# Which queue issues the first loads: both first x tiles and a quarter of Wq from ScalarE, and eight V stores moved behind Wo's loads

## The chip, the cores and the metric

The kernel runs on one core of a Trainium2 chip. The core has TensorE (PE, matrix products), VectorE (DVE), ScalarE (ACT), GpSimd (POOL) and SyncE (SP). SyncE, ScalarE and GpSimd can issue DMAs; each has a queue of its own, and the 16 DMA engines of the core serve all of them. The metric is the device time of one execution in microseconds (us), lower is better. Unless another unit is given, numbers in the text are microseconds, and points in time are counted from the start of the profiled span.

## The reference

A segment-recurrent attention block, then a gated block with spatial mixing, on one sequence of S = 2048 rows, width 512, 32 heads of 128, 64 segments of 32 rows, and 8 memory rows that each segment hands to the next:

```python
x = layernorm(A_x)
mem = mem0
for s in range(64):
    h = concat([mem, x[:, 32*s:32*s+32]])          # 40 rows
    q, k, v = h @ Wq, h @ Wk, h @ Wv               # 32 heads of 128
    p = softmax(where(mask, q @ k.T * 128**-0.5, -1e9))
    o = sum over heads of (p @ v) @ Wo
    mem = o[:, :8]
    outs.append(o[:, 8:])
h = A_x + concat(outs)
z = gelu(layernorm(h) @ w_in)
g = w_sp @ layernorm(z[:, 896:]) + b_sp
out = h + (z[:, :896] * g) @ w_out
```

## The kernel before

The program is recorded operation by operation by a small emitter. It keeps one list for each engine, in the order in which the calls are made, and works out from tokens (names of buffers that an operation reads or writes) which semaphore each one waits for. So the order of the calls is the order on each engine, and a DMA stands in the queue of the engine whose list it was added to (`sp(...)` for SyncE, `em.add("act", ..., dma=True)` for ScalarE, `"pool"` for GpSimd). These parts are enough to follow what is said below:

- **First loads** (lines 300 to 323). `load_xe(ck, j)` (L300) loads an "x end" tile of 128 x 512 in bf16: the last 8 rows of each of the 16 segments of chunk `ck`. `load_x(rb, j)` (L292) loads a block of 128 rows of x. `load_w(mi, hq, queues)` (L310) loads quarter `hq` (8 heads, 1 MB) of Wq, Wk or Wv (`mi` 0, 1, 2); with two queues named it is cut into two halves of 512 columns, each a DMA of its own with a token of its own, so that readers of the first four heads wait for the first half alone. A row of a half is 1 KB for each of 4 x 128 descriptors, a row of a whole quarter 2 KB. L315 loads ScalarE's table for exp and ln.
- **The start of the work** (lines 797 to 848). 34 small matmuls warm TensorE up (`warm`, L794). The two x tiles get their layernorm: statistics of both on VectorE (L363, L364), then the scale (L373). The first is transposed on TensorE (L383) and copied to `hTe` by ScalarE (L407). Then come 16 groups of `start_x` (L445): `start_x(ck, i)` gives q of the segment ends of chunk `ck` for heads 4i to 4i + 3 (i below 8; from 8 on it gives k). The order is `start_x(0, 0)`, the transposes of the second tile, then `start_x(0, 1)`, `start_x(1, 0)`, `start_x(0, 2)`, `start_x(1, 1)` and so on. `start_x(0, 0)` and `start_x(1, 0)` read the first half of Wq's first quarter, `start_x(0, 1)` and `start_x(1, 1)` the second half, each further pair of i one more quarter. PSUM results go alternately through ScalarE (L461) and VectorE (L463).
- **The batched V groups** (L472). Eight groups `start_v(n)` give v of the segment ends of chunk 0. `vx_evac` (L476 to L490) copies a group to `part[n]` (L484 on ScalarE for odd n, L486 on VectorE for even n) and stores it to DRAM (`vext_d`) in two pieces: the first 16 of its 128 rows, which segments 0 and 1 need, from ScalarE's or GpSimd's queue, and the other 112 rows from SyncE's queue. The `part` buffers are written again by `part_evac` (L684) from segment 0 on, and that has to wait for the stores.
- **Wo's loads** (L852): four DMAs of 1 MB on SyncE's queue, with no wait of their own. They are read by L672 from the end of segment 0 on.
- **The segments** (from L940): 64 rounds. `load_vx(s)` (L497) fetches the stored V rows of one segment, for segments 0 and 1 from GpSimd's queue; for the others SyncE does it, two segments ahead, and waits for all 16 store pieces. The rows are used in L645.

After the segments come the second block's products (L1163 spatial mixing, L1258 output).

Of the kernel before, what the change touches and what calls it, by code (L numbers as in the profile page):

```python
# [169 lines left out]
def fast_path(nc, st, keep, A_x, A_mem0, A_Wq, A_Wk, A_Wv, A_Wo, A_seg_len, B_w_in, B_w_sp, B_b_sp, B_w_out, out):  # L170
# [25 lines left out]
    em = Emitter(n_dma_sems=40)  # L196
# [71 lines left out]
    def PB(b):  # L268
        return ("ps", b)

    def sp(fn, **k):
        return em.add("sp", fn, dma=True, **k)
# [4 lines left out]
    def act(fn, **k):  # L277
        return em.add("act", fn, **k)

    def dve(fn, **k):  # L280
        return em.add("dve", fn, **k)
# [8 lines left out]
    def load_x(rb, j):  # L290
        t, tok = xbuf(j)
        sp(lambda e: e.dma_start(t, xr[:, rb, :]), writes=tok)  # L292


    def xbuf(j):
        return (xn[:, j, :], [("xn", j)]) if j < 2 else (part[:, j, :], [("part", j, 0), ("part", j, 1)])

    def load_xe(ck, j, queue="sp"):
        t, tok = xbuf(j)
        em.add(queue, lambda e: e.dma_start(t, xe[CK * ck:CK * ck + CK, XM:SEG, :]), dma=True, writes=tok)  # L300

    def load_w(mi, hq, queues=("sp",)):
        parts = len(queues)
        wd, ws = ((A_Wq, w_q), (A_Wk, w_k), (A_Wv, w_v))[mi]
        wr = wd.rearrange("(dc p) h e -> p dc (h e)", p=128)
        n = 8 * DH // parts
        for k in range(parts):
            c0, c1 = hq * 8 * DH + k * n, hq * 8 * DH + (k + 1) * n
            tok = ("W", mi, hq) if k == parts - 1 else ("W", mi, hq, k)
            em.add(queues[k], lambda e, c0=c0, c1=c1: e.dma_start(ws[:, :, c0:c1], wr[:, :, c0:c1]), dma=True, writes=[tok])  # L310
            em.mark_const(tok)

    load_xe(0, 0)
    load_xe(1, 1, "act")
    act(lambda e: e.preload_act_table_set("natural_log_exp_and_others"))  # L315
    load_w(0, 0, ("sp", "sp"))
    load_w(0, 1, ("act",))
    load_w(0, 2)
    load_w(0, 3, ("act",))
    load_x(0, 4)  # L320
    load_x(1, 5)
    load_xe(2, 6)
# [153 lines left out]
    def vx_evac(ck, n, bank, eng="act", queue="sp"):  # L476
        if ck == 0:
            t, tok = part[:, n, :], [("part", n, 0), ("part", n, 1)]
        else:
            j = vcnt[0] % 2  # L480
            vcnt[0] += 1
            t, tok = Vs[:, j, :], [("Vs", j)]
        if eng == "act":
            act(lambda e: e.activation(out=t, in_=ps[:, bank, :], func=ACT.Copy, scale=VSC), reads=[PB(bank)], writes=tok)  # L484
        else:
            dve(lambda e: e.tensor_scalar(out=t, in0=ps[:, bank, :], scalar1=VSC, scalar2=None, op0=ALU.mult), reads=[PB(bank)], writes=tok)  # L486
        for k, (i0, i1) in enumerate(((0, 2), (2, CK)) if ck == 0 else ((0, CK),)):
            r = slice(8 * i0, 8 * i1)
            dst = vext_d[ck, n, r, :, :].rearrange("p r e -> p (r e)")
            em.add("sp" if k else queue, lambda e, r=r, dst=dst: e.dma_start(dst, t[r, :]), dma=True, reads=tok, writes=[("vext", ck, n, k)])  # L490

    vcnt = [0]
    NVL = 2

    def load_vx(s, queue="sp"):
# [278 lines left out]
    def zp_evac(rb, hf, bank, eng):  # L774
        j = zpc[0] % 2
        zpc[0] += 1
        t = Vs[:, j, 0:HF]
        if eng == "act":
            act(lambda e: e.activation(out=t, in_=ps[:, bank, 0:HF], func=ACT.Copy), reads=[PB(bank)], writes=[("Vs", j)])
        else:  # L780
            dve(lambda e: e.tensor_copy(out=t, in_=ps[:, bank, 0:HF]), reads=[PB(bank)], writes=[("Vs", j)])
        sp(lambda e: e.dma_start(zp_d[rb, :, hf * HF:(hf + 1) * HF], t), reads=[("Vs", j)], writes=[("zpd", rb, hf)])
# [39 lines left out]
    def start_v(n, ck=0):  # L822
        start_group(vx_mm, vx_evac, ck, n)
# [27 lines left out]
    for hq in range(4):  # L851
        sp(lambda e, hq=hq: e.dma_start(w_o[:, 8 * hq:8 * hq + 8, :], wor[:, 8 * hq:8 * hq + 8, :]), writes=[("Wo", hq)])  # L852
        em.mark_const(("Wo", hq))

    class Gap:
        def __init__(self):
# [22 lines left out]
    def vx_group(ck, n):  # L879
        gx.append([lambda dc=dc: vx_mm(ck, n, XB, dc) for dc in range(DC)] + [lambda: vx_evac(ck, n, XB, "dve")])  # L880

    def vx_atoms(ck, n):
        mms = [lambda ck=ck, n=n, dc=dc: vx_mm(ck, n, VXB, dc) for dc in range(DC)]
        gv.add(VXB, mms, lambda eng: vx_evac(ck, n, VXB, eng))
# [55 lines left out]
    for s in range(NSEG):  # L940
# [89 lines left out]
        if s == 3 * CK + 1:  # L1030
            for r, hf in zgap:
                gv.add(VXB, [lambda r=r, hf=hf, dc=dc: zp_mm(r, hf, VXB, (dc,)) for dc in range(DC)],
                       lambda eng, r=r, hf=hf: zp_evac(r, hf, VXB, eng))
# [142 lines left out]
    def zbank():  # L1176
        zcnt[0] += 1
        return 5 + zcnt[0] % 3
# [26 lines left out]
    for i, rb in enumerate(order):  # L1205
# [23 lines left out]
        if i in (3, 4):  # L1229
            r, j, bank = RB - 5 + i, i % 2, zbank()  # L1230
# [729 lines left out]
def build_kernel(nc, A_x, A_mem0, A_Wq, A_Wk, A_Wv, A_Wo, A_seg_len, B_x, B_w_in, B_w_sp, B_b_sp, B_w_out, out):  # L1960
    args = (A_x, A_mem0, A_Wq, A_Wk, A_Wv, A_Wo, A_seg_len, B_w_in, B_w_sp, B_b_sp, B_w_out, out)
    with contextlib.ExitStack() as keep:
        with contextlib.ExitStack() as st:
            em, sems, dsems, flag = fast_path(nc, st, keep, *args)
# [88 lines left out]
```

## Time and profile before

| | |
|---|---|
| device time, median of 3 runs (lowest to highest) | 863.92 us (863.6 to 864.41) |
| the profiled execution | 861.39 us |
| its span, first to last instruction | 859.8 us |
| mean granted TensorE clock | 0.995 |
| busy: PE, ACT, DVE, POOL | 98%, 57%, 53%, 19% of the span |
| DMA | 76.09 MB, mean 88 GB/s; 327 and 385 GB/s in the first two slices of 21.5 us |

How to read it: in the timeline a row has its start, its length (of several merged instructions from the first start to the last end), the engine, the line of the kernel, the operation, what it writes and reads, how many were merged, and in brackets the idle time of the engine before it with what ended that. "SPq" and "ACTq" are DMA issues on SyncE's and ScalarE's queue; the length is that of the issuing instruction, not of the transfer. Matmuls are pipelined, so a busy TensorE is not one at its peak. In the table of DMA queues a row has the queue, its packets, its MB and the time that its packets took as a share of 16 engines' time; q1 is SyncE's queue, q10 ScalarE's, q0 GpSimd's.

### The profile page before, as it was taken

What the parts mean: (1) busy time and instruction counts of PE and PEld (TensorE: products, weight loads), DVE (VectorE), ACT (ScalarE), POOL (GpSimd) and SP (SyncE); (2) the same over time, 40 slices, a digit from 0 to 9 for tenths busy, and PEclk for the clock granted to TensorE, in tenths of its full rate; (3) what the DMA queues carried; (4) which work ended last, traced back from release to release, by engine and by line L of the source; (5) the groups of instructions that cost most, each with busy time, mean ns of one, the idle gap of its engine ahead of it and who ended that gap; (6) DMA issues with size and microseconds to landing.
All of it is one profiled execution on the core that took longest, in us unless ns stands there. A gap on an engine that the chain in (4) does not pass through costs nothing.

```text
span 859.8 us, 48647 instructions
## 1 busy us (share of the span) xinstructions
PE 843.7 (98%) x22466; PEld 495.2 (58%) x22466; DVE 455.2 (53%) x1031; ACT 492.8 (57%) x1309; POOL 160.0 (19%) x409
## 2 busy tenths in 40 slices
PE   7999999999999999999999999999999999999997
PEld 7755665566565665656565556565665544444443
DVE  3545545555555555565556555555555466563443
ACT  2466676766776676667776667666666676300000
POOL 4212112111221111111211121112211123200000
PEclk8999999999999999999999999999999999999999
DMA  9972212131312230213112120433332289023001
GB/s 327 385 217 68 66 47 59 48 77 32 71 39 43 57 78 24 70 55 65 58 49 69 25 78 26 119 70 75 69 76 63 68 249 318 1 98 107 35 13 47
DMA packets 95730, 76.09 MB, mean 88 GB/s; under 512 B 46040, under 2 KB 81504, under 8 KB 95520
## 3 DMA queue, kind: packets, MB, share of 16 engines
q1 hardware_dynamic: 93632, 70.09, 28.6%
q8 instruction: 178, 2.92, 1.5%
q10 hardware_dynamic: 1616, 2.49, 0.8%
q0 software_dynamic: 272, 0.33, 0.1%
q14 instruction: 32, 0.26, 0.1%
HBM read 41.75 MB, written 20.91 MB: 73 GB/s over the span
## 4 chain that ended last, share of the span: by engine, by line
PE 95%; DMA 2%; SPq 1%; ACT 1%; DVE 1%; issue 0%; ACTq 0%; POOL 0%; DVEq 0%; POOLq 0%
PE f_ps L523 26%; PE f_ps L672 13%; PE f_ps L618 13%; PE f_ps L1163 11%; PE f_ps L422 4%; PE f_ps L472 4%; PE f_ps L717 3%; PE f_ps L1258 3%; PE f_ps L638 3%; PE f_ps L445 2%; PE f_ps L563 2%; PE f_ps L768 2%; PE f_ps L1156 2%; DMA f_arena<-in_A_Wq_dram 1%; PE f_ps L555 1%; PE f_ps L584 1%
## 5 line engine op out<-in xcount | busy, mean ns | idle before, releaser
L523 PE MATMUL f_ps<-f_arena,f_hT 128*32 128x512 bf16 (+1 forms) x5120 | 241.1, 337 | 0.2
L534 ACT ACTIVATE f_Tst<-f_ps 128x512 bf16<-128x512 f32 (+1 forms) x320 | 150.1, 510 | 46.8 <-PE f_ps L523 40.3
L523 PEld LDWEIGHTS f_ps<-f_arena,f_hT 128*32 128x32 bf16 x5120 | 119.8, 96 | 93.0 <-ACT f_hT L695 34.8
L618 PE MATMUL f_ps<-f_arena,f_hT 128*32 128x512 bf16 x2048 | 139.0, 379 | 0.0
L672 PE MATMUL f_ps<-f_arena,f_cT 128*32 128x256 bf16 x4096 | 128.3, 272 | 1.2 <-issue 1.0
L608 POOL TENSOR_TENSOR f_E_sb<-f_R_sb,f_E_sb 128x64 bf16<-128x64 f32 x128 | 52.7, 412 | 380.6 <-ACT f_R_sb L600 380.6
L542 DVE STREAM_TRANSPOSE f_QT<-f_Tst 128x256 uint32<-128x256 uint32 x128 | 57.0, 445 | 124.0 <-ACT f_Tst L534 124.0
L672 PEld LDWEIGHTS f_ps<-f_arena,f_cT 128*32 128x32 bf16 x4096 | 99.7, 96 | 23.8 <-ACT f_cT L658 20.5
L1163 PE MATMUL f_ps<-f_arena 128*128 128x512 bf16 x448 | 100.6, 379 | 0.6 <-DMA f_arena<-wT_d 0.6
L660 DVE TENSOR_SCALAR f_cT<-f_ps 128x320 bf16<-128x320 f32 x128 | 56.9, 486 | 46.3 <-PE f_ps L645 46.3
L1163 PEld LDWEIGHTS f_ps<-f_arena 128*128 128x128 bf16 x448 | 43.7, 98 | 53.1 <-DMA f_arena<-wT_d 0.7
L684 ACT ACTIVATE f_part<-f_ps 128x256 bf16<-128x256 f32 x128 | 49.2, 384 | 39.6 <-PE f_ps L672 37.3
L542 DVE STREAM_TRANSPOSE f_KT<-f_Tst 128x128 uint32<-128x128 uint32 (+1 forms) x192 | 65.8, 343 | 7.0 <-ACT f_Tst L534 2.9
L630 DVE TENSOR_SCALAR f_V_sb<-f_ps 128x512 bf16<-128x512 f32 x64 | 44.3, 692 | 47.1 <-PE f_ps L618 47.1
L658 ACT ACTIVATE f_cT<-f_ps 128x320 bf16<-128x320 f32 x128 | 49.0, 435 | 34.2 <-PE f_ps L645 34.2
L577 ACT ACTIVATE f_E_sb<-f_ps 128x224 bf16<-128x224 f32 x128 | 45.4, 354 | 35.0 <-PE f_ps L569 34.1
L604 DVE TENSOR_TENSOR f_E_sb<-f_R_sb,f_E_sb 128x160 bf16<-128x160 f32 x128 | 41.7, 325 | 18.5 <-ACT f_R_sb L600 18.5
L695 ACT ACTIVATE f_hT<-f_ps 128x16 bf16<-128x16 f32 x126 | 23.2, 184 | 45.0 <-PE f_ps L692 45.0
L618 PEld LDWEIGHTS f_ps<-f_arena,f_hT 128*32 128x32 bf16 x2048 | 40.0, 96 | 14.8 <-issue 0.3
L1169 DVE TENSOR_TENSOR f_arena<-f_ps,f_arena 128x512 f32<-128x512 f32 x28 | 19.3, 690 | 52.7 <-PE f_ps L1163 52.7
L600 ACT ACTIVATE f_R_sb<-f_R_sb 128x160 f32<-128x160 f32 x128 | 43.1, 337 | 4.5 <-ACT f_Vs L484 0.4
L422 PE MATMUL f_ps<-f_arena,f_hTe 128*32 128x512 bf16 x640 | 41.6, 379 | 0.0
(124 smaller groups left out, 1152.7 us busy)
## 6 DMA issues: line engine op xcount, KB each, us to landing
wT_d<-f_wst SPq DMA_DIRECT2D x32, 256.0 KB, 3.7
f_arena<-wT_d SPq DMA_DIRECT2D x32, 256.0 KB, 5.5
f_arena<-in_A_Wv_dram SPq DMA_DIRECT2D x4, 1024.0 KB, 11.8
f_arena<-in_A_Wk_dram SPq DMA_DIRECT2D x4, 1024.0 KB
f_arena<-in_A_Wo_dram SPq DMA_DIRECT2D x4, 1024.0 KB, 12.0
f_Vx<-vext_d SPq DMA_DIRECT2D x62, 64.0 KB
vext_d<-f_Vs SPq DMA_DIRECT2D x22, 128.0 KB, 2.0
zp_d<-f_Vs SPq DMA_DIRECT2D x20, 112.0 KB, 2.1
```

The costliest lines, as they stand in the source:

```text
L422: pe(lambda e, c=c, rhs=rhs: e.matmul(ps[32 * c:32 * c + 32, bank, :], lhsT=hTe[:, ck, dc, 32 * sg:32 * sg + 32], rhs=rhs, start=(dc == 0) ...
L523: pe(lambda e, dc=dc, c=c, rhs=rhs: e.matmul(ps[32 * c:32 * c + 32, bank, 0:32 * nh], lhsT=hT[:, sl, dc, :], rhs=rhs, start=(dc == 0), sto ...
L534: act(lambda e: e.activation(out=st_.rearrange("p (hp i r) -> p hp i r", i=32, r=2), in_=ps[:, bank, 0:64 * np_].rearrange("p (hp r i) -> ...
L542: dve(lambda e: e.transpose(out=dst, in_=src), reads=tok, writes=[(nm, b, k) for k in halves(b, p0, np_)])
L577: act(lambda e: e.activation(out=E_sb[:, b, :], in_=ps[:, bank, 0:224], func=ACT.Exp, scale=scale, bias=SHIFT), reads=[PB(bank)], writes=[ ...
L608: pool(lambda e: e.tensor_tensor(out=ev, in0=rv, in1=ev, op=ALU.mult), reads=[("R", b), ("Ex", b)], writes=[("Ex", b)])
L618: pe(lambda e, dc=dc, c=c, c0=c0: e.matmul(ps[32 * c:32 * c + 32, bank, 0:w], lhsT=hT[:, sl, dc, :], rhs=w_v[:, dc, c0:c0 + w], start=(dc ...
L658: act(lambda e: e.activation(out=dst, in_=src, func=ACT.Copy, scale=UNSC), reads=[PB(PVB[c])], writes=[("cT", c)])
L660: dve(lambda e: e.tensor_scalar(out=dst, in0=src, scalar1=UNSC, scalar2=None, op0=ALU.mult), reads=[PB(PVB[c])], writes=[("cT", c)])
L672: pe(lambda e, h=h, g=g, i=i, b=b, c=c: e.matmul(ps[32 * g:32 * g + 32, bank, 0:d1 - d0], lhsT=cTh[:, i, 8:40], rhs=w_o[:, h, d0:d1], star ...
L684: act(lambda e: e.activation(out=part[:, s % 8, d0:d1], in_=ps[:, bank, 0:d1 - d0], func=ACT.Copy), reads=[PB(bank)], writes=[("part", s % ...
L1163: pe(lambda e: e.matmul(ps[:, bank, 0:TB], lhsT=z2[:, sc, fb * 128:(fb + 1) * 128], rhs=wTb[tb % 2][:, :, sc, :], start=first, stop=last), ...
```

## The change

Two things are changed. The products, their order on TensorE, VectorE, ScalarE and GpSimd, and the bytes that are moved are the same.

First, the first loads. Before, SyncE's queue had x tile 0, the two halves of Wq's first quarter, and Wq's third quarter; ScalarE's queue had x tile 1, the table load, Wq's second and fourth quarter. Now ScalarE's queue has x tile 0, x tile 1, the two halves of Wq's first quarter, and then the table load; SyncE's queue starts with Wq's second, third and fourth quarter. What follows on SyncE's queue (three more x blocks, `mem0`, Wv, Wk) keeps its order.

Second, the 112-row stores of the V groups. They are put on a list (`vrest`) when the group is copied and are added to SyncE's queue behind Wo's four loads. The 16-row stores are where they were.

```diff
-    load_xe(0, 0)
+    load_xe(0, 0, "act")
     load_xe(1, 1, "act")
+    load_w(0, 0, ("act", "act"))
     act(lambda e: e.preload_act_table_set("natural_log_exp_and_others"))
-    load_w(0, 0, ("sp", "sp"))
-    load_w(0, 1, ("act",))
-    load_w(0, 2)
-    load_w(0, 3, ("act",))
+    for hq in range(1, 4):
+        load_w(0, hq)
     load_x(0, 4)
     load_x(1, 5)
     load_xe(2, 6)
...
-            em.add("sp" if k else queue, lambda e, r=r, dst=dst: e.dma_start(dst, t[r, :]), dma=True, reads=tok, writes=[("vext", ck, n, k)])
-
-    vcnt = [0]
+            if k:
+                vrest.append(lambda r=r, dst=dst: sp(lambda e: e.dma_start(dst, t[r, :]), reads=tok, writes=[("vext", ck, n, 1)]))
+            else:
+                em.add(queue, lambda e, r=r, dst=dst: e.dma_start(dst, t[r, :]), dma=True, reads=tok, writes=[("vext", ck, n, 0)])
+
+    vcnt, vrest = [0], []
...
     for hq in range(4):
         sp(lambda e, hq=hq: e.dma_start(w_o[:, 8 * hq:8 * hq + 8, :], wor[:, 8 * hq:8 * hq + 8, :]), writes=[("Wo", hq)])
         em.mark_const(("Wo", hq))
+    for f in vrest:
+        f()
```

## The prediction

> **What bounds the kernel now.** I read the page first, then the chain of waits, then the timeline of the start, the packets of each DMA queue in short windows, and the granted clock by window.
>
> ```profile
> span 859.8 us, 48647 instructions
> ...
> PE 95%; DMA 2%; SPq 1%; ACT 1%; DVE 1%; issue 0%; ACTq 0%; POOL 0%; DVEq 0%; POOLq 0%
> ```
>
> The chain that ended last runs on TensorE for 95% of the span; 2% of it are DMAs. The chain in order of time shows the long one:
>
> ```profile
> 1.56 9.46 DMA f_arena<-in_A_Wq_dram
> ...
> 28.79 7.02 PE f_ps L472 x128
> ```
>
> So the transfer on the path is the first half of Wq's first quarter (I call the halves Wq0a and Wq0b), on its way from 1.56 to 11.02. The change touches the start only, and what it does to the start is carried to the end: in that chain no other DMA stands between 11.02 and the V groups (L472). The timeline of the start:
>
> ```profile
> 0.81 0.69 SPq L300 DMA_DIRECT2D f_xn<-in_A_x_dram  x1
> 0.82 0.67 ACTq L300 DMA_DIRECT2D f_xn<-in_A_x_dram  x1
> 1.56 1.11 ACTq L310 DMA_DIRECT2D f_arena<-in_A_Wq_dram  x2
> 1.56 1.98 SPq L310 DMA_DIRECT2D f_arena<-in_A_Wq_dram  x3
> 4.00 0.69 DVE L363 BATCH_NORM_STATS2 f_st<-f_xn 128x6 f32<-128x512 bf16 x1 [4.00 <-DMA f_xn<-in_A_x_dram]
> 4.83 0.66 DVE L363 BATCH_NORM_STATS2 f_st<-f_xn 128x6 f32<-128x512 bf16 x1
> 6.82 0.60 ACT L407 ACTIVATE f_hTe<-f_ps 128x512 bf16<-128x512 bf16 x1 [4.02 <-PE f_ps L383]
> 11.15 1.87 PE L445 MATMUL f_ps<-f_hTe,f_arena 128*128 128x128 bf16 x16 [3.82 <-DMA f_arena<-in_A_Wq_dram]
> 13.24 13.80 PE L445 MATMUL f_ps<-f_hTe,f_arena 128*128 128x128 bf16 x224
> ```
>
> Two x tiles go to VectorE's statistics (both, before the first is applied), the first tile's transpose is ready at 6.82 + 0.60 = 7.42, and TensorE then waits 3.7 us for Wq0a. The first group (16 matmuls, heads 0 to 3) takes 1.87 us; after the second tile's transposes the second group starts at 13.24. That one reads heads 4 to 7, so it needs **Wq0b**, and from there 224 matmuls run without a hole. So 13.24 is the time to beat, and the transfer that decides it after the change is Wq0b, not Wq0a.
>
> **How the queues share.** Packets by queue (q10 is ScalarE's, q1 SyncE's), in the windows 2 to 3.5, 3.5 to 5, 7 to 10, 11 to 12 and 0 to 12 us, in this order:
>
> ```profile
> q10 hardware_dynamic: 154, 0.15, 54.6%
> q1 hardware_dynamic: 127, 0.12, 23.0%
> ...
> q10 hardware_dynamic: 238, 0.49, 90.1%
> q1 hardware_dynamic: 17, 0.01, 2.3%
> ...
> q10 hardware_dynamic: 371, 0.76, 69.5%
> q1 hardware_dynamic: 371, 0.37, 36.8%
> ...
> q1 hardware_dynamic: 328, 0.34, 105.2%
> ...
> q10 hardware_dynamic: 1200, 2.23, 53.9%
> q1 hardware_dynamic: 1194, 1.19, 29.6%
> ```
>
> By 12 us ScalarE's queue has moved its 1200 packets: an x tile of 128, two quarters of 512 (2 KB each), 16 small ones for each of three DMAs. SyncE's three first DMAs are also 128 + 512 + 512 + 48 = 1200, of 1 KB, and 1194 are through. Three things follow. With both queues busy they take packets one for one, 371 / 3 = 124 per us each, so the queue with 1 KB rows gets half the bytes of the other. Alone, SyncE's queue moved 328 per us. And SyncE moved 127 + 17 = 144 packets up to 5.0, exactly its x tile: not one packet of Wq0a, issued at 1.56, moved before 5.0, while ScalarE's Wq1 took 238 packets. A DMA that came just behind the other queue's megabyte was **held for 3.4 us**.
>
> The Trainium skill (DMA: Bandwidth & Descriptors, Issuing engines are not separate DMA queues) says that spreading DMAs over issuing engines saves only the sequencer's issue time, since all run on the same 16 engines. By that rule alone the regrouping would be worth nothing and the time would stay at 863.9. This trace agrees on the total rate, but not on when one transfer lands: the one-for-one packets and the 3.4 us decide that.
>
> **The change, first part.** ScalarE's queue gets, in order, x tile 0, x tile 1, Wq0a, Wq0b: 2 x 144 + 2 x 528 = 1344 packets of 1 KB. SyncE's gets Wq1, Wq2, Wq3 and then all else; it never runs dry while ScalarE's list lasts, so the last stretch at 328 per us, which Wq0b had, is gone. Bounds for Wq0b, with data beginning at about 2.3 as now (154 packets by 3.5 at 124 per us):
> - even share from the first packet: 2.3 + 1344 / 124 = 13.1, and 0.4 to the semaphore (x tile 0's last packets moved just after 3.5, VectorE started at 4.00) = 13.5: 0.3 us late against 13.24.
> - x tile 1 held behind SyncE's Wq1 as Wq0a was behind ScalarE's: its issue ends some 0.67 after 0.82, so 1.49 + 3.4 = 4.9; then 144 + 1056 = 1200 packets, 9.7 us, to 14.6, and 0.4: 15.0, **1.8 us late**. Wq0a would be there at 4.9 + 672 / 124 + 0.4 = 10.7; the tile's statistics start near 6.5 instead of 4.83 and the transpose is ready 2.6 us later, 9.1, still ahead of it.
> - two of SyncE's megabytes ahead of it: one more costs 528 packets at 238 / 1.5 = 159 per us, 3.3 us, or the 2 us that Wq1 kept Wq0a out after data began at 3: 3.8 to 5.1 us late.
>
> I take the second: it is the one case in the trace of a small transfer meeting the other queue's megabyte. What hides: the table load on ScalarE moves behind four issues (2 x 0.67 + 1.11 us from 0.82, so about 3.3 to 4.6) and is done 2 us before 6.82; Wq1 and Wq3 are through after 528 and 3 x 528 packets at 124 per us, about 7 and 15.6, and are first read two and ten groups of 13.80 / 14 = 1 us behind 13.24; the tiles for later groups carry the same bytes ahead of them as now.
>
> **The clock.**
>
> ```profile
> 6.62 0.72 PE L794 MATMUL f_ps<-f_onesrc 128*128 128x160 bf16 x8
> ...
> 8.00:9.00 1.00, 0.00 (x0) 0.00 (x0) 0.00 (x0) 0.00 (x0) 0.72 (x4) 0.89 1.05 368
> 14.00:15.00 1.00, 1.00 (x12) 1.00 (x11) 0.00 (x0) 0.08 (x1) 0.79 (x4) 0.50 1.06 380
> 15.00:16.00 1.00, 1.00 (x16) 1.00 (x14) 0.00 (x0) 0.78 (x2) 0.80 (x4) 0.70 1.13 394
> ```
>
> The first row is the timeline's, the others are windows, where the column before the last two is the granted clock: half speed from about 8.8 to 15.6. Behind 13.24 that costs (15.6 - 13.24) / 2 = 1.2 us now. After the change TensorE works from 10.7 to 13.2, pauses to 15.0, and starts again. At best it runs at full speed then (1.2 us gained), at worst it needs the 4.45 us from 11.15 to 15.6 once more (2.2 lost, 1.0 more than now). I take +0.3, nearer the worst, because a pause stands right ahead of the long run.
>
> The Trainium skill (TensorE: Matmul & The Clock Gate, Part 1) has the gate fall after a whole idle window of about 3.4 us. By that the 1.8 us pause costs nothing and the sum would be 0.3 less. Here the clock fell at 8.8 although TensorE had worked from 6.62 to 7.34, so I keep the row's value.
>
> **The change, second part.**
>
> ```profile
> 16.61 11.29 SPq L310 DMA_DIRECT2D f_arena<-in_A_Wk_dram  x4
> 30.54 6.25 SPq L490 DMA_DIRECT2D vext_d<-f_part  x8
> 31.30 0.38 ACTq L490 DMA_DIRECT2D vext_d<-f_part  x1
> 32.40 0.60 ACT L484 ACTIVATE f_part<-f_ps 128x512 bf16<-128x512 f32 x1 [1.13 <-PE f_ps L472]
> 36.83 8.52 SPq L852 DMA_DIRECT2D f_arena<-in_A_Wo_dram  x4
> 41.93 1.25 POOL L497 DMA_DIRECT2D f_Vx<-vext_d  x2 [5.06 <-DMA vext_d<-f_part]
> ...
> f_arena<-in_A_Wo_dram SPq DMA_DIRECT2D x4, 1024.0 KB, 12.0
> ...
> L852 SPq DMA_DIRECT2D f_arena<-in_A_Wo_dram x4: 446/2546/2859, 36.8 to 42.5; - x4
> ...
> f_Vx<-vext_d POOLq DMA_DIRECT2D x2, 64.0 KB, 6.7
> ...
> 54.02 0.21 PE L645 MATMUL f_ps<-f_E_sb,f_Vx 32*128 32x64 bf16 x4
> 55.36 1.94 PE L672 MATMUL f_ps<-f_arena,f_cT 128*32 128x256 bf16 x56
> 56.68 0.38 ACT L684 ACTIVATE f_part<-f_ps 128x256 bf16<-128x256 f32 x1 [1.12 <-PE f_ps L672]
> ...
> 54.00:56.00 2.00, 1.79 (x68) 1.03 (x58) 1.35 (x4) 0.77 (x2) 0.96 (x3) 1.00 0.41 135
> ```
>
> Timeline, DMA issues (with Wo's line), timeline again, and one window. Today SyncE issues eight second-row stores (112 rows of 1 KB, 0.115 MB each) from 30.54 and Wo's four loads only at 36.83; afterwards Wo goes out behind Wk's issues, which end at 27.9, and the stores follow. Nothing is added; the engines stay busy until about 55 either way (share 0.41 in 54 to 56). Wo's last quarter, issued at 42.5 with 12.0 to land, arrives at about 54.5 against L672's start at 55.36, so today it has less than 1 us in hand; ahead of 8 x 0.115 MB at 0.34 MB per us (11 to 12 us above) it comes 2.7 us sooner. No wait goes away: 0. The stores end at about 55. The first frees a buffer that ScalarE writes at 56.68, and it lands some 2.5 us ahead of the others: covered by 3 to 4 us, a wait of that size if the cover goes. The small V loads on GpSimd (41.93 + 6.7 = 48.6, used at 54.02) have 5 us in hand. I cost this part at 0.
>
> **Sum.** Against the profiled execution (861.39, span 859.8) 1.8 + 0.3 gives 863.5. The median of the three runs, 863.92, stands 2.5 above that execution, and I add the same 2.1 to it: 863.92 + 2.1 = **866.0**.
>
> **Rivals.**
> - *Even share*: +0.3, and the clock between -1.2 and +1.0: 863.0 to 865.2, likeliest 864.2, no change. For it: one-for-one packets whenever both queues run. Against: the 3.4 us. It is also what the skill's rule on issuing engines comes to.
> - *ScalarE's list runs ahead*: faster. In the trace ScalarE's DMAs got in first both times (154 packets against 127, 238 against 17). Were its whole list through before SyncE's megabytes, x at 288 / 120 per us ends at 4.7, Wq0a and Wq0b at 4.7 + 1056 / 328 = 7.9; then the second x tile, 5.1 + 2.6 = 7.7, starts the first group and the second one follows 1.87 + 0.6 later, at 10.2: 3.0 us won, 860.9, with Wo's 2.7 us needed to keep it. Against: SyncE's queue starts with a megabyte at the same instant. It decides if Wq0b lands before about 11.
> - *Two megabytes ahead*, +3.8 to +5.1: 867.7 to 869.
> - *ScalarE's issue is held up*: its four first-row stores (0.38 each at 31.30 and later) now issue while SyncE's Wo loads fill the queues, which took SyncE 8.52 / 4 = 2.1 us each. At 2.1, ScalarE loses 4 x 1.75 = 7 us, with 1.13 us idle ahead of each evacuation to absorb it: 7 - 4 x 1.13 = 2.5 us late on top of the forecast, 868.5.
>
> **Chances.** Forecast 0.38; even share 0.30; ScalarE ahead 0.15; the last two 0.17 together. What this kernel's runs can tell from no change is about 0.2%, 1.7 us. Even share falls within it; of the forecast (its own range 864.5 to 867) about 0.27 is beyond 865.65 and the rest within; the last two are slower. So faster 0.15, same 0.40, slower 0.45. The range 862.0 to 869.0 leaves out ScalarE ahead and the far end of the last two.
>
> **What would show it.** In the profile after: the second statistics instruction starts near 6.5 (even share: below 5.3; two megabytes: 8 or more); the first group near 10.7; a pause of TensorE behind the second tile's transposes until about 15; ScalarE's queue 124 packets per us from 5 to 14; Wo issued from about 28; no TensorE wait at L645, L672 or behind L684. If the second group starts before 13, or the small stores' issues take 2 us, I am wrong in that step; if it starts at 15 and the time still does not move, the start is not what sets the end.

## The result, and the profile after

| | before | after |
|---|---|---|
| device time, median (lowest to highest), 22 runs of each, side by side | 864.26 us (861.3 to 867.3) | 867.05 us (864.4 to 870.85) |
| ratio after / before, 95% interval | | 1.0035 [1.0023, 1.0047] |
| the profiled execution, its span | 861.39, 859.8 us | 867.73, 865.9 us |
| mean granted TensorE clock | 0.995 | 0.991 |

The changed kernel is slower, by 0.0035 x 864.26 = 3.0 us. Single executions of one kernel lie 6 us apart in both columns, and up to 8 us in the runs below, so totals are compared by ratios of many runs below, and traces by when TensorE reaches a given place.

The page of after has a chain of the same kind as before. The first line is the span; the other gives the chain's share by engine:

```profile
span 865.9 us, 48647 instructions
...
PE 95%; DMA 1%; DVE 1%; ACT 1%; issue 0%; ACTq 0%; POOL 0%; DVEq 0%; POOLq 0%
```

The first two long pieces of that chain, in order of time (start, length, what):

```profile
2.99 12.90 DMA f_arena<-in_A_Wq_dram
15.94 15.29 PE f_ps L444 x224
```

The transfer on the path is now the **second** half of Wq's first quarter (Wq0b). It ends at 2.99 + 12.90 = 15.89, and the second group of `start_x` starts 0.05 later. Before, the chain held the first half, until 11.02. The timeline of after (the lines have moved by one or two: L444 is L445 of before, L471 is L472, L362 is L363, L406 is L407, L854 is L852):

```profile
0.81 1.56 SPq L310 DMA_DIRECT2D f_arena<-in_A_Wq_dram  x3
0.81 1.30 ACTq L300 DMA_DIRECT2D f_xn<-in_A_x_dram  x2
2.15 1.43 ACTq L310 DMA_DIRECT2D f_arena<-in_A_Wq_dram  x2
6.85 0.69 DVE L362 BATCH_NORM_STATS2 f_st<-f_xn 128x6 f32<-128x512 bf16 x1 [6.85 <-DMA f_xn<-in_A_x_dram]
7.83 0.69 DVE L362 BATCH_NORM_STATS2 f_st<-f_xn 128x6 f32<-128x512 bf16 x1
9.87 0.60 ACT L406 ACTIVATE f_hTe<-f_ps 128x512 bf16<-128x512 bf16 x1 [4.98 <-PE f_ps L382]
12.33 1.87 PE L444 MATMUL f_ps<-f_hTe,f_arena 128*128 128x128 bf16 x16 [1.43 <-DMA f_arena<-in_A_Wq_dram]
15.94 15.29 PE L444 MATMUL f_ps<-f_hTe,f_arena 128*128 128x128 bf16 x224 [1.32 <-DMA f_arena<-in_A_Wq_dram]
...
27.93 14.85 SPq L854 DMA_DIRECT2D f_arena<-in_A_Wo_dram  x4
...
35.49 0.35 ACTq L492 DMA_DIRECT2D vext_d<-f_part  x1
...
59.54 1.70 PE L674 MATMUL f_ps<-f_arena,f_cT 128*32 128x256 bf16 x56
```

Read it from the top. Both queues issue at 0.81, and ScalarE's x tiles are the first in its queue. Yet the first tile's statistics start at 6.85 where they started at 4.00, and the brackets name the x DMA: **both** tiles are late. The second group starts at 15.94, 2.70 behind 13.24. From the Wo row on nothing is worse: Wo is issued from 27.93, ScalarE's small store takes 0.35 to issue, and TensorE enters L674 without a wait.

The packets of each queue (q10 ScalarE's, q1 SyncE's; packets, MB, share of 16 engines' time), in the windows 2 to 3.5, 3.5 to 5, 7 to 10 and 0 to 16:

```profile
q1 hardware_dynamic: 137, 0.28, 68.2%
...
q1 hardware_dynamic: 275, 0.56, 100.9%
q10 hardware_dynamic: 23, 0.02, 4.4%
...
q1 hardware_dynamic: 377, 0.75, 70.9%
q10 hardware_dynamic: 359, 0.36, 35.8%
...
q1 hardware_dynamic: 2086, 3.66, 65.6%
q10 hardware_dynamic: 1344, 1.31, 24.4%
```

In the first window ScalarE's queue has no row at all, and between 2 and 5.0 it has moved 23 packets against SyncE's 137 + 275 = 412. SyncE's Wq1 is ahead of the x tiles, although those were issued no later. From 7 to 10 both queues go one for one, 359 / 3 = 120 per us. ScalarE's list is 1344 packets long, as was counted from the code.

The granted clock (the column before the last two), by windows of after:

```profile
7.00:8.00 1.00, 0.00 (x0) 0.00 (x0) 0.90 (x3) 0.00 (x0) 0.15 (x1) 0.90 1.07 359
8.00:9.00 1.00, 0.00 (x0) 0.00 (x0) 0.95 (x3) 0.00 (x0) 0.76 (x3) 0.50 1.05 368
20.00:21.00 1.00, 1.00 (x12) 1.00 (x11) 0.46 (x2) 0.00 (x0) 0.39 (x2) 0.50 1.05 387
21.00:22.00 1.00, 1.00 (x17) 1.00 (x15) 0.00 (x0) 0.69 (x2) 0.00 (x0) 0.78 1.05 389
```

A mean of 0.90 between 7 and 8 is full speed for 0.8 us and half for 0.2: half clock from 7.8. The 0.78 puts its end at 21.4. It lasted 13.6 us, against 6.8 before.

### The profile page after: what moved, and what is told of

Its sections match the earlier page's. It is cut to its first block, busy times and chain, and to the rows that moved or that the text cites. A ratio compares the mean times of both kernels' runs of the same rounds, so it can differ in the third digit from the quotient of the medians.

```text
span 865.9 us, 48647 instructions
## 1 busy us (share of the span) xinstructions
PE 847.0 (98%) x22466; PEld 498.8 (58%) x22466; DVE 455.3 (53%) x1031; ACT 492.8 (57%) x1309; POOL 159.6 (18%) x409
## 4 chain that ended last, share of the span: by engine, by line
PE 95%; DMA 1%; DVE 1%; ACT 1%; issue 0%; ACTq 0%; POOL 0%; DVEq 0%; POOLq 0%
PE f_ps L525 26%; PE f_ps L674 13%; PE f_ps L620 13%; PE f_ps L1168 11%; PE f_ps L421 4%; PE f_ps L471 4%; PE f_ps L719 3%; PE f_ps L1263 3%; PE f_ps L640 2%; PE f_ps L444 2%; PE f_ps L565 2%; PE f_ps L1161 2%; PE f_ps L770 2%; DMA f_arena<-in_A_Wq_dram 1%; PE f_ps L1128 1%; PE f_ps L557 1%
## 5 line engine op out<-in xcount | busy, mean ns | idle before, releaser
L674 PE MATMUL f_ps<-f_arena,f_cT 128*32 128x256 bf16 x4096 | 128.3, 273 | 0.6 <-issue 0.3
L674 PEld LDWEIGHTS f_ps<-f_arena,f_cT 128*32 128x32 bf16 x4096 | 100.2, 96 | 22.7 <-ACT f_cT L660 19.8
L1168 PEld LDWEIGHTS f_ps<-f_arena 128*128 128x128 bf16 x448 | 43.7, 98 | 52.6 <-DMA f_arena<-wT_d 0.2
L686 ACT ACTIVATE f_part<-f_ps 128x256 bf16<-128x256 f32 x128 | 49.0, 383 | 39.3 <-PE f_ps L674 37.0
## 6 DMA issues: line engine op xcount, KB each, us to landing
f_arena<-in_A_Wv_dram SPq DMA_DIRECT2D x4, 1024.0 KB, 13.6
```

The costliest lines, as they stand in the source:

```text
L674: pe(lambda e, h=h, g=g, i=i, b=b, c=c: e.matmul(ps[32 * g:32 * g + 32, bank, 0:d1 - d0], lhsT=cTh[:, i, 8:40], rhs=w_o[:, h, d0:d1], star ...
L686: act(lambda e: e.activation(out=part[:, s % 8, d0:d1], in_=ps[:, bank, 0:d1 - d0], func=ACT.Copy), reads=[PB(bank)], writes=[("part", s % ...
L1168: pe(lambda e: e.matmul(ps[:, bank, 0:TB], lhsT=z2[:, sc, fb * 128:(fb + 1) * 128], rhs=wTb[tb % 2][:, :, sc, :], start=first, stop=last), ...
```

## The experiments

My theory was that a queue whose megabyte gets in first keeps the other queue's small DMAs out, so that the x tiles and then Wq's first quarter are late; nothing else in the change counts. Rivals: the stores' new place costs the time, the sheer sharing of packets does, or the granted clock does. Each ratio is the run's time over that of the kernel before on the same chip.

**Each part alone.** First the new first loads, with the stores in front of Wo as before:

```diff
-            if k:
-                vrest.append(lambda r=r, dst=dst: sp(...))
-            else:
-                em.add(queue, lambda e, r=r, dst=dst: e.dma_start(dst, t[r, :]), ...)
+            em.add("sp" if k else queue, lambda e, r=r, dst=dst: e.dma_start(dst, t[r, :]), ...)
...
-    for f in vrest:
-        f()
```

> The first part of the change alone (first loads regrouped, V stores in front of Wo as before). My theory, that the whole loss is in the first part: the second group of q products starts at 15.9 as in the changed kernel (13.24 before), the V groups at about 33 (28.8 before), the time is 1.0035 of before within 0.0015. Rival, that the stores behind Wo cost time: second group at 15.9 too, but the time is nearer to before, 1.001 or less. Rival, that the stores behind Wo win time back that the first part loses: 1.005 or more.

Measured: 867.63 against 863.35, ratio 1.0049 [1.0032, 1.0065]. Statistics at 6.82, second group at 15.98, V groups at 32.87: the start of after.

Then the old first loads, with the stores behind Wo:

```diff
-    load_xe(0, 0, "act")
+    load_xe(0, 0)
     load_xe(1, 1, "act")
-    load_w(0, 0, ("act", "act"))
     act(lambda e: e.preload_act_table_set("natural_log_exp_and_others"))
-    for hq in range(1, 4):
-        load_w(0, hq)
+    load_w(0, 0, ("sp", "sp"))
+    load_w(0, 1, ("act",))
+    load_w(0, 2)
+    load_w(0, 3, ("act",))
```

> The second part alone (first loads as before, the eight stores behind Wo's loads). My theory: nothing, ratio 1.000 within 0.0015, second group at 13.2, no wait of TensorE at the products that read Wo or the stored V rows. Rival, the stores behind Wo cost: 1.002 or more, with a wait of ScalarE for a buffer or of TensorE for V rows between 50 and 60 us. Rival, Wo's earlier arrival wins: 0.998 or less.

Measured: 863.29 against 863.35, ratio 0.9996 [0.9983, 1.0008]. The whole loss is in the first loads; with the old loads the stores' place is worth nothing that the interval shows. Whether the stores win a little back behind the late start (the first run's 1.0049 against 1.0035) the intervals do not tell. The second group started at 12.68 here, and the V groups at 27.80, with the same first loads that gave 13.24 and 28.72 in the profile of before. So one execution's start is good to about half a us, and its V groups to about 1 us.

**Take the megabyte away from the tiles.** Changed kernel, but SyncE issues Wq1 only when both x tiles have landed. The queues and the order in each are those of after:

```diff
     act(lambda e: e.preload_act_table_set("natural_log_exp_and_others"))
+    em.add("sp", None, after=[em.last_w[("xn", 0)], em.last_w[("xn", 1)]])
     for hq in range(1, 4):
```

> The changed kernel, queues and lists unchanged, but SyncE's first quarter of Wq is issued only when both x tiles have landed. Holding theory: nothing holds ScalarE's list now, the x tiles land at 3.6 to 4.2, Wq0a moves alone and lands at 5.5 to 6.5, Wq0b shares one for one only from about 5.5 on and lands at 9 to 10.5; the second group starts by 10.7, 5 us sooner than in the changed kernel, and the time is 0.994 to 0.998 of before, though every other load starts 3 us later. Rival, even share from the first packet: at most the x tiles' 288 packets are saved, the second group starts at 13 to 13.6. Rival, that the later start of all other loads decides: TensorE waits for Wq1, Wv or Wk and the time is 1.000 or more.

Measured: 862.07 against 864.58, ratio 0.997 [0.9957, 0.9984], the lowest ratio of all that were run, though its interval overlaps those of several runs below. Its timeline (here the lines are those of before):

```profile
3.49 0.70 DVE L363 BATCH_NORM_STATS2 f_st<-f_xn 128x6 f32<-128x512 bf16 x1 [3.49 <-DMA f_xn<-in_A_x_dram]
5.73 1.56 SPq L310 DMA_DIRECT2D f_arena<-in_A_Wq_dram  x3
5.74 0.69 DVE L363 BATCH_NORM_STATS2 f_st<-f_xn 128x6 f32<-128x512 bf16 x1 [1.33 <-DMA f_xn<-in_A_x_dram]
...
8.27 1.91 PE L445 MATMUL f_ps<-f_hTe,f_arena 128*128 128x128 bf16 x16
10.41 2.08 PE L445 MATMUL f_ps<-f_hTe,f_arena 128*128 128x128 bf16 x32
13.21 10.89 PE L445 MATMUL f_ps<-f_hTe,f_arena 128*128 128x128 bf16 x192 [0.72 <-DMA f_arena<-in_A_Wq_dram]
26.35 3.64 PE L472 MATMUL f_ps<-f_arena,f_hTe 128*32 128x512 bf16 x64
31.38 2.99 PE L472 MATMUL f_ps<-f_arena,f_hTe 128*32 128x512 bf16 x52 [1.40 <-issue]
```

The only thing taken away is the megabytes that start beside the tiles, and the first tile is there at 3.49 in place of 6.85: that is the hold. The second tile is a miss: it was expected by 4.2 and was used at 5.74, although SyncE had issued nothing. Of the 16 landings that the trace has for it nine had come by 4.63 and the last came at 5.71, and seven single packets of 1 KB, begun from 3.39 to 3.57, took 1.3 to 1.7 us each, where most take 0.05; what slowed them is not shown. Wq0a followed at 7.64, not at 5.5 to 6.5. The second group starts at 10.41, 5.5 earlier than in after, and needs no wait for Wq. That 5.5 has two things in it, which this run does not separate: the hold is gone, and until 5.7 nothing shares the engines with ScalarE's list. SyncE's data is 4.9 late in return, which shows as a wait of 0.72 in front of L445 at 13.21 and as 1.40 in the middle of the V groups: the row names only "issue" there, but by the trace's landings the last quarter of Wv arrived at 31.29, 0.09 ahead of the matmuls' start.

**Move one tile back.** Changed kernel, with x tile 0 as SyncE's first DMA again:

```diff
-    load_xe(0, 0, "act")
+    load_xe(0, 0)
```

> The changed kernel with x tile 0 back on SyncE's queue; ScalarE's queue then has x tile 1, Wq0a, Wq0b, SyncE's x tile 0, Wq1, Wq2, Wq3. Holding theory (the DMA that gets in first keeps the other queue's out): both queues start with an x tile, so both land near 4.0 as before, and Wq0a and Wq1 meet as second DMAs as Wq1 and Wq0a did before, where ScalarE's got in first. Then Wq0a lands at 6 to 8 and Wq0b at 10 to 12.5, the second group starts before 12.7 and the kernel is 1 to 3 us faster than before. If SyncE's gets in first, Wq0a is held to 5.0 and the second group starts at 13.5 to 14. Rival, even share only: 3.3 + 1056/124 + 0.4 = 12.2 for Wq0b whoever is first.

Measured: 862.15, ratio 0.9981 [0.9966, 0.9997]. Its timeline, and its packets between 3.5 and 5:

```profile
4.32 0.69 DVE L362 BATCH_NORM_STATS2 f_st<-f_xn 128x6 f32<-128x512 bf16 x1 [4.32 <-DMA f_xn<-in_A_x_dram]
8.17 1.91 PE L444 MATMUL f_ps<-f_hTe,f_arena 128*128 128x128 bf16 x16
11.62 12.68 PE L444 MATMUL f_ps<-f_hTe,f_arena 128*128 128x128 bf16 x224 [1.31 <-DMA f_arena<-in_A_Wq_dram]
```

```profile
q10 hardware_dynamic: 467, 0.47, 88.7%
q1 hardware_dynamic: 51, 0.06, 11.5%
```

One tile of 144 packets in front of SyncE's first megabyte turns the hold round. Now ScalarE's queue, with Wq's first quarter, takes 467 packets and SyncE's 51; in after it was 23 to 275. The same list of weights is held or let through by which queue gets in first. What decides that between two weight loads is not shown: here ScalarE's was issued at 1.52 and SyncE's at 1.56.

**Small loads first.** Changed kernel, with SyncE's three x blocks and `mem0` in front of its megabytes instead of behind:

```diff
-    for hq in range(1, 4):
-        load_w(0, hq)
     load_x(0, 4)
     load_x(1, 5)
     load_xe(2, 6)
     sp(lambda e: e.dma_start(m0, A_mem0[0]), writes=[("xo", 0)])
+    for hq in range(1, 4):
+        load_w(0, hq)
```

> The changed kernel with SyncE's four small loads (three x blocks and mem0, some 0.4 MB) in front of its three quarters of Wq. Holding theory (ScalarE's first tiles wait until the descriptors of SyncE's first DMA are out, a time that goes with its size): SyncE's first DMA is now 128 packets instead of 512, so the x tiles land 1.5 to 2.5 us sooner than in the changed kernel (first statistics at 4.3 to 5.3 instead of 6.85) and the second group starts at 13.5 to 14.5 instead of 15.9. Rival, that only the even share of packets counts: no packet of the list in front of Wq0b is saved, the second group starts at 15.5 to 16 and the time stays at 1.0035.

Measured: 864.43, ratio 1.0019 [1.0000, 1.0039]. Its timeline:

```profile
3.65 0.69 DVE L362 BATCH_NORM_STATS2 f_st<-f_xn 128x6 f32<-128x512 bf16 x1 [3.65 <-DMA f_xn<-in_A_x_dram]
7.11 0.69 DVE L362 BATCH_NORM_STATS2 f_st<-f_xn 128x6 f32<-128x512 bf16 x1 [2.54 <-DMA f_xn<-in_A_x_dram]
10.57 1.86 PE L444 MATMUL f_ps<-f_hTe,f_arena 128*128 128x128 bf16 x16 [0.52 <-DMA f_arena<-in_A_Wq_dram]
14.70 14.31 PE L444 MATMUL f_ps<-f_hTe,f_arena 128*128 128x128 bf16 x224 [1.84 <-DMA f_arena<-in_A_Wq_dram]
```

The first tile is free at 3.65, sooner than the 4.3 to 5.3 expected, but the second comes at 7.11, little earlier than behind the megabyte (7.83), and the second group at 14.70 misses the forecast by 0.2. Small DMAs ahead of the megabytes free the first tile only. Of the second tile's 16 landings in the trace 15 had come by 4.29 and the last came at 7.09. As in the run where SyncE waits, in which the second tile was late with nothing beside it, this is not the hold by the other queue's megabyte, and its cause is not shown.

**Does an earlier start last?** The loads of the one-tile kernel, with the stores in front of Wo again (the stores' own lines go back as in the first run):

```diff
-    load_xe(0, 0, "act")
+    load_xe(0, 0)
...
-    for f in vrest:
-        f()
```

> The loads of e4_x0_on_sp (second group at 11.62, V groups at 25.98) with the eight stores back in front of Wo's loads. Theory, that the stores' place matters only if the start gets earlier: Wo's last quarter lands near 54.5 to 55 as before, L672's products want it 2.7 us sooner than 55.36, so TensorE waits 1.5 to 2.5 us there and the time is 1.000 of before, against 0.998 of e4_x0_on_sp. Rival, that the stores' place never matters: no such wait, and the time as e4_x0_on_sp.

Measured: 863.3 against 864.58, ratio 0.9989 [0.9975, 1.0002]. Its V groups start at 26.93, 1.79 earlier than before's; by 58 its profile is 1.56 behind that of before. Its table of waits (engine, line, releaser: total, times, longest) and one window:

```profile
PE f_ps L671 <- DMA f_arena<-in_A_Wo_dram: 0.9, 1, 0.9
```

```profile
57.00:58.00 1.00, 1.00 (x24) 0.78 (x20) 0.00 (x0) 0.39 (x1) 0.00 (x0) 0.50 0.40 131
```

TensorE, now earlier, waits 0.80 at 54.65 for something that the row does not name and 0.87 at 55.94 for Wo, less than the 1.5 to 2.5 expected of Wo, and its clock falls to half: 3.35 lost between 52.6 and 58.4. With the stores behind Wo (the one-tile kernel) the V groups were 2.74 earlier than before's, and 2.27 of it was left at 58. So in these two profiles the second part of the change has a use once the start is earlier. The totals, 0.9989 and 0.9981, lie too near each other to show it.

**A still earlier start.** x tile 0 and Wq0b on SyncE, x tile 1 and Wq0a on ScalarE:

```diff
-    load_xe(0, 0, "act")
+    load_xe(0, 0)
     load_xe(1, 1, "act")
-    load_w(0, 0, ("act", "act"))
+    load_w(0, 0, ("act", "sp"))
```

> x tile 0 and Wq0b from SyncE's queue, x tile 1 and Wq0a from ScalarE's, then all else from SyncE's; stores behind Wo. Holding theory: the x tiles land near 4, Wq0a goes first (done near 5.8 as in e4_x0_on_sp), Wq0b follows with nothing beside it and lands by 7 to 8. Then the first group starts at 7.5 to 8, right behind the first tile's copy, the second group at 9.2 to 10.5 without a wait for a load, and the time is 0.994 to 0.997 of before (3 to 5 us), unless Wv's last quarters (about 28.8) hold the V groups. Even-share rival: Wq0b shares with Wq0a and then has the queue behind it, also about 8; it differs only in Wq0a, 8 instead of 6.

Measured: 862.86, ratio 0.998 [0.9965, 0.9994], less than forecast. The start is the earliest of all (first group 7.65, second 8.78, no wait for Wq), V groups at 24.62. Then come two waits:

```profile
53.10 2.88 PE L674 MATMUL f_ps<-f_arena,f_cT 128*32 128x256 bf16 x52 [0.86 <-issue]
```

The first, 0.52 in the middle of the V groups, ends at 28.78, and by the trace the last quarter of Wv had landed at 28.69: there the weights set a second limit behind the first. The other is the 0.86 in this row, inside Wo's product. The row names no DMA, and Wo's last quarter had landed at 52.23, so this wait is not for Wo; its cause is not shown. The clock is at half from 53.24 to 56.65. Of 4.1 us won by 25, 1.0 was left at 58.

**The clock.** Changed kernel, with more of the small matmuls that keep TensorE busy and whose results nobody reads:

```diff
-    warm(34)
+    warm(60)
...
-    warm(8)
+    warm(18)
...
     xe_copy(1, 7)
+    warm(8)
```

> The changed kernel with 44 more of the warming matmuls (26 ahead of the first tile's transposes, 10 behind them, 8 behind the second tile's transposes), so that TensorE stays busy while it waits for the loads. The second group is still set by Wq0b: 15.9. Theory, that the clock adds to the late transfer: with the clock up before 15.9 the 224 matmuls take about 12.7 instead of 15.29, the V groups start near 30.4 instead of 32.9, and the time is 1.5 to 2.7 us below the changed kernel, ratio to before 1.000 to 1.002. Rival, that the late transfer is all: no change of the V groups against 32.9 beyond 0.5 us.

Measured: 867.52, ratio 1.0041 [1.0022, 1.006], from five runs: the clock never fell in its profile, V groups at 30.32, but no gain in time. As that was few runs, the changed kernel and the warmed one were timed once more side by side:

> The changed kernel itself, timed again beside the next run on one chip, to settle what the half clock costs it. Its profile so far has half clock from 7.80 to 21.45, and its median is 1.0035 of the kernel before. Theory A (the half clock in the start is part of the loss): ratio 1.0025 to 1.0055, and 2.0 to 3.0 us (0.002 to 0.0035) above the warmed kernel of the next run. Theory B (the clock's share is given back later, so that only the transfer counts): both at the same ratio within 0.001.

> The warmed kernel (60, 18 and 8 small matmuls more in TensorE's holes, which compute nothing that is used) again, with more rounds than before. Its profile kept full clock from 3.85, and the V groups started at 30.32 instead of 32.90, 2.6 us earlier. Theory A: a ratio of 0.9995 to 1.0025 to the kernel before, 2.0 to 3.0 us below the changed kernel of this call. Theory B: the same ratio as the changed kernel within 0.001, that is 1.003 to 1.005, because the 2.6 us are lost again in the segments.

Measured: changed kernel 867.3, ratio 1.0042 [1.0029, 1.0054]; warmed 868.08, ratio 1.0048 [1.0033, 1.0063]. The timeline of the changed kernel, taken again, and below it that of the warmed one:

```profile
15.86 13.96 PE L444 MATMUL f_ps<-f_hTe,f_arena 128*128 128x128 bf16 x224 [1.32 <-DMA f_arena<-in_A_Wq_dram]
...
31.50 3.85 PE L471 MATMUL f_ps<-f_arena,f_hTe 128*32 128x512 bf16 x68
```

```profile
15.93 12.68 PE L444 MATMUL f_ps<-f_hTe,f_arena 128*128 128x128 bf16 x224 [1.80 <-DMA f_arena<-in_A_Wq_dram]
...
30.29 4.07 PE L471 MATMUL f_ps<-f_arena,f_hTe 128*32 128x512 bf16 x72
```

224 matmuls take 12.68 at full clock; the changed kernel took 13.96 here and 15.29 in its first profile, with the same transfer. So the start won by warming is 1.2 or 2.6, but the medians do not show it: 1.0048 and 1.0042 are within theory B's 0.001, and theory A's 2 us are not there. To see whether the added instructions cost it, the kernel before got the same ones:

```diff
-    warm(34)
+    warm(60)
...
-    warm(8)
+    warm(18)
...
     xe_copy(1, 7)
+    warm(8)
```

> The kernel before, with the same added small matmuls as the warmed kernel (60, 18 and 8 in place of 34, 8 and none; they compute nothing that is used). In the kernel before the half clock lay from 8.77 to 15.60, of which 1.2 us fell on useful work behind 13.24 and 0.9 us on the first group. Theory C (the added instructions cost nothing, the clock counts): full clock in the start, V groups 1 to 2 us earlier (26.7 to 27.7 for 28.72), ratio 0.9975 to 0.999. Theory D (the added instructions cost some 2 to 3 us later, in short waits of TensorE in the segments, which is why the warmed version of the changed kernel did not gain): V groups as early as by C, but a ratio of 1.0005 to 1.003.

Measured: 863.42 against 864.48, ratio 0.9995 [0.998, 1.0009], between the two theories. V groups at 27.04, as by C. Its timeline, and one window:

```profile
27.04 7.09 PE L472 MATMUL f_ps<-f_arena,f_hTe 128*32 128x512 bf16 x128
...
54.71 2.54 PE L672 MATMUL f_ps<-f_arena,f_cT 128*32 128x256 bf16 x44 [0.52 <-DMA f_arena<-in_A_Wo_dram]
```

```profile
56.00:57.00 1.00, 1.00 (x24) 0.76 (x20) 0.12 (x1) 0.38 (x1) 0.00 (x0) 0.50 0.00 1
```

The 1.68 us won at 27 are lost around 55 as in the run with the stores in front of Wo: a wait of 0.52 for Wo, and half clock from 54.6 to 58.0. That fits this run, but not the warmed changed kernel, whose clock stays full at 55. Where that one gives its gain back **stays open**; between 60 and 605 its profile falls 4.5 us behind that of before in short waits spread over the segments, without a single large one. That is no mark of the warming alone: in the same stretch the profile of the run where SyncE waits falls 3.3 behind, that of the one-tile kernel 2.9, that of the changed kernel 1.8. The profile of before was a fast execution (861.39, median 864.26), so one profile against it cannot place such a loss.

## Why the prediction was right, and where its sizes were off

The time came out at 867.05 for 866.0 forecast, slower, by the mechanism that was chosen. By its steps:

- **The hold.** Right, and shown by three runs: with the megabyte out of the way the first tile is at 3.49, with the megabyte beside it at 6.85, and one tile in front of SyncE's megabyte reverses who is held. Mis-sized is the step "x tile 1 held", with tile 0 in time. Both were held: the two queues issued at the same instant, and I took ScalarE's first DMA to be in first as in the trace of before, where both queues began with a tile. So statistics start at 6.85 and 7.83, where the second was forecast near 6.5; the first group at 12.33, not 10.7; Wq0b at 15.89, not 15.0. Tile 0's 144 packets, held as well, are 1.2 us at 120 per us, which covers the 0.9 by which Wq0b came later. The term "+1.8" measured +2.7 in the profiles of before and after, and by the 12.68 of the run with the old loads it could be 3.3. How much of it is the hold and how much the one-for-one sharing, no run separates.
- **One for one, and the list's length.** Right: 359 and 377 packets in 3 us, 120 per us against 124, and 1344 in all.
- **Wq0b decides.** Right: the chain has it, and the pause behind the second tile's transposes ends with it.
- **Clock, +0.3.** Against 12.68 at full clock, half clock cost the 224 matmuls 13.80 - 12.68 = 1.1 before, and 2.6 or 1.3 after, in its two profiles: +1.5 or +0.2. My upper bound of +1.0 came from the 4.45 us of work that ended the half clock before; after, it lasted from 12.33, the start of work, to 21.4. Whether any of this reaches the total is not shown, since the warmed kernel did not gain.
- **Second part, 0.** Right: 0.9996 alone. Wo was issued from 27.93 (28 forecast), with no wait at L647 or L674 or behind L686, and the issues by ScalarE took 0.35, so the rival "ScalarE's issue is held up", which needed 2.1, is out.
- **Even share** needed the second group before 13.5; it falls with 15.94. **Two megabytes ahead** needed the second statistics at 8 or more and Wq0b 3.8 to 5.1 late; 7.83 and 2.7 are short of it, though nearer than I gave it credit for. **ScalarE's list ahead** did not happen in after. It happened by half in the run with tile 0 on SyncE: Wq0a had landed by 5.8, but Wq0b shared one for one and was there at 11.6, not 7.9, and the time was 862.15 where I had 860.9. That Wo's earlier loads would be needed to keep it is what the profile of the run with the stores in front of Wo showed.

The sum of 2.1 met 3.0 in the ratio. That it came so near is in part luck: the transfer was 0.9 to 1.5 too small, the V groups of the two profiles of after start 4.2 and 2.8 behind 28.72, and what the clock adds to the total is not known.

The Trainium skill (DMA: Bandwidth & Descriptors, Queues, rings and completion order) says that each DMA engine takes turns between the queues it has work for, a packet at a time, and that such a packet is typically some 9 to 17 descriptors and at most 64. The window from 7 to 10 agrees with turns (359 to 377). In the first ones the second queue gets no turn for long: none to 137, then 23 to 275, and 467 to 51 when the other queue is first. A packet of the profile's rows is one row of 1 or 2 KB here, which is one descriptor, so SyncE's 412 are about 26 for each of the 16 engines. That is more than the typical turn of the Trainium skill and less than its largest; no run here shows how long a turn is. By turns of single rows the x tiles' 288 packets would have been through 2.4 us after the first data (288 / 120, an estimate from the rows).

## What to carry to other kernels

When two queues start together, look at which one has a small DMA in front: a megabyte that gets in first can keep the other queue's small loads out (the first tile came at 6.85 instead of 3.49 here), so start the megabytes behind the loads that the first work needs, or with a wait for them, which gave the lowest ratio here, 0.997. Find the transfer that the long run of work waits for (here the second half of a quarter, not the first) and count what is moved ahead of it in its own queue and, one for one, in the other. An earlier start is kept only as far as the next load is earlier too: here waits for Wv or Wo, one wait of unknown cause, and the half clock behind them left 1.0 of 4.1 us in one profile and nothing of 1.8 in another.

## What the runs showed that was not expected

- The hold goes either way and is decided by 144 packets. With SyncE's Wq1 first, ScalarE moved 23 packets up to 5.0; with a tile in front of it, ScalarE moved 172 + 467 in the same time (172 from 2 to 3.5).
- Half clock in the start lasted 6.8 in before, 13.6 in one profile of the changed kernel; the other profile had the 224 matmuls in 13.96 instead of 15.29 with the transfer at the same place. It came back at 15.6 and 21.4, not with the start of work but at the end of 3.4 us in which TensorE worked without a hole (12.2 to 15.6, and 18.0 to 21.4). In other profiles it lasted 3.4 (the run where SyncE waits) and 10.2 (small loads first, and the changed kernel again). The Trainium skill (TensorE: Matmul & The Clock Gate, Part 1) has the clock decided in windows of about 3.4 us that run free of the kernel, which agrees with these lengths of one to four such windows.
- A wait of only 0.5 to 0.9 in segment 0 comes with half clock in three runs (around 53 to 59), and together they cost 2.0 to 3.4 us. It need not: the one-tile kernel has a wait of 0.48 there (53.41) and full clock.
